# A Fourier mixer on one core: the channel transform as two products of 512 columns instead of four of 257, its evacuation given priority, and two products in one PSUM bank

## The chip, the cores and the metric

The kernel runs on one core of a Trainium2 chip. The metric is the device time of one execution in microseconds (us). The engines are TensorE (PE; PEld is its weight load), VectorE (DVE), ScalarE (ACT), GpSimd (POOL) and the DMA queues, most of them issued by SyncE (SP). PE writes its results to PSUM, which has eight banks of 512 float32 columns on 128 partitions; ACT and DVE read them from there ("evacuate").

## What is computed

Three stages follow each other; B = 8 batches, 576 positions, 512 channels (8 heads of 64).

```python
p_packed = sm_attn(p, k, v)                  # 32 queries per head over 576 positions
x = sm_attn(q, p_packed, p_packed)           # 576 queries per head over the 32

X = np.fft.fft(np.fft.fft(x, axis=1), axis=2)     # sequence, then channels
u = x + np.real(X)
un = (u - mean(u)) / np.sqrt(var(u) + 1e-6)
x2 = u + np.maximum(un @ w_ch1, 0) @ w_ch2        # 512 -> 2048 -> 512

logits = x2 @ w_gate                         # 8 experts, one chosen for each position
out = p[e] * (np.maximum(x2 @ w1[e], 0) @ w2[e])
```

Float32 accuracy is reached with float16 matmuls: a value is split in a high and a low half (hi = float16(v), lo = v - hi), and a product is three matmuls, hi*hi, hi*lo and lo*hi (PASS).

## The kernel before, in words

The generator attention(b) does the first stage and the Fourier transform of batch b, Mix the two dense layers of the second stage (L741 makes hp from ut and w1h, L749 evacuates it to ht, L761 adds w2h times ht to acc), and from about 900 us on the experts run. While Mix works on one group of tokens, attention(b) of the next batch and the splitting of the expert weights (se, so; L306 to L308) are ticked on in small steps between Mix's matmuls. Each engine works through its own instructions in order; a scheduler places them in that order at build time by priorities, and tc.high_priority moves an operation ahead (URGENT and SOON are offsets for that). A tile that an operation needs is waited for by semaphore.

The real part of a two-dimensional transform is made without the transform of x itself. x = A p_packed, with A the attention weights of 576 positions over 32 packed rows for each head, so the channel transform is applied to p_packed (256 rows of it, in two halves hf), and the sequence transform to A:

- channels(k), L466 to L477: g = p_packed times a constant table cdt of cosines (cs = 0, 257 columns) and sines (cs = 1, 257 columns). For each of four (hf, cs) a PSUM tile gp is filled by six matmuls (three passes, two halves of 64 rows), ACT casts it to float16 (L475) and DVE makes the low half (L476).
- scores2 to parts2, L484 to L547: the second attention, in three row tiles i; s is the score tile, ee the exponentials, m the sums and their reciprocals, t a partial sum made on POOL (L512), ah the split for the direct path, eo the even and odd combinations (L532 to L536) and eh their halves (L542 to L546).
- L552: a list of thirteen steps tells which of these are issued together; channels(0) to channels(3) stand in the sixth, eighth, tenth and twelfth.
- bp, L558 to L571: the sequence transform of eh, in four PSUM tiles, evacuated to bt, a part of the tile big.
- L583 to L662: for each of three row tiles t, P = bt times the cosine part of g, Q = bt times the sine part, and X, the direct attention output. ACT copies Q to qs (L634), DVE adds P and qs into ul and uu (L638 to L651) and X to those (L660). For t = 2, which has only 32 rows, P and Q already share a bank on different partitions.

All of s, gp, lp (the gate logits of earlier tokens), bp, zd, P, Q and X take their PSUM tile from one pool of two banks, in turn (psA, tag "att"; in batch 0 two of three such tiles come from another pool). So a product may begin when the tile two before it has been read:

```python
psA = ctx.enter_context(tc.tile_pool(name="psA", bufs=2, space=PSUM))
def att(nm):
    return psA.tile([128, 512], F32, tag="att", name=nm)
```

Of the kernel before, what the change touches and what calls it, by code (L numbers as in the profile page):

```python
# [8 lines left out]
F32 = mybir.dt.float32  # L9
F16 = mybir.dt.float16  # L10
I32 = mybir.dt.int32
AF = mybir.ActivationFunctionType
ALU = mybir.AluOpType
# [35 lines left out]
def prep(inputs):  # L49

    f = np.float32
    q, k, v, p = (np.asarray(inputs[n]) for n in "qkvp")
# [11 lines left out]
    o = {}  # L64
# [26 lines left out]
    def split(a):  # L91
        hi = a.astype(np.float16)
        return hi, (a - hi.astype(np.float64)).astype(np.float16)

    n = np.arange(288)[:, None]
# [26 lines left out]
    o["c3"] = c3  # L122
    c = tau[:, None]
    k2 = np.arange(257)[None, :]
    cd = np.concatenate([np.cos(2 * np.pi * ((c * k2) % 512) / 512), np.sin(2 * np.pi * ((c * k2) % 512) / 512)], 1)
    cd = np.stack(split(cd), 1)
    o["cdt"] = np.ascontiguousarray(cd.reshape(4, 128, 2, 514).transpose(1, 0, 2, 3))
    pp = np.arange(128)
    c16 = np.zeros((128, 4, 128), np.float16)
    c16[:, 0] = pp[:, None] < pp[None, :]  # L130
# [23 lines left out]
def build(tc, A, stop=None, manual=False):  # L154
    nc = tc.nc
    with ExitStack() as ctx:
        if manual:
            ctx.enter_context(tc.manual_schedule())
        _build(tc, nc, ctx, A, stop)
# [4 lines left out]
URGENT = 100  # L164
# [15 lines left out]
def _build(tc, nc, ctx, A, stop):  # L180
# [10 lines left out]
    ap = actx.enter_context(tc.tile_pool(name="ap", bufs=1, side="left"))  # L191
# [17 lines left out]
    nc.scalar.activation(warm, mhalf[0:1], AF.Exp)  # L209
    cst = ap.tile([128, 10, 290], F16, name="cst")  # L210
    c3 = ap.tile([128, 3], F32, name="c3")
    cdt = ap.tile([128, 4, 2, 514], F16, name="cdt")
    c16 = cp.tile([128, 4, 128], F16, name="c16")
    i32r = cp.tile([128, 32], F16, name="i32r")
    i32v = cp.tile([128, 32], F16, name="i32v")
# [7 lines left out]
    zt = ap.tile([128, 2, 2, 128], F16, name="zt")  # L223
# [91 lines left out]
    def attention(b):  # L315
        count = [0]

        def att(nm):
            count[0] += 1
            if b == 0 and count[0] % 3:  # L320
                return psO.tile([128, 512], F32, tag="o", name=nm)
            return psA.tile([128, 512], F32, tag="att", name=nm)
# [88 lines left out]
        for hf in range(2):  # L411
# [13 lines left out]
            n = 0  # L425
            for t in range(5):
                for (x, y) in PASS:
                    for h in range(2):
# [3 lines left out]
                                         skip_group_check=True)  # L432
# [28 lines left out]
        bt = big[:, 2304:].rearrange("p (h a c n) -> p h a c n", h=2, a=2, c=2)  # L461
        aeo = []

        g = ap.tile([128, 2, 2, 2, 257], F16, tag="g", name=f"g{b}")

        def channels(k):  # L466
            hf, cs = k % 2, k // 2
            gp = att(f"gp{b}_{k}")
            for n, (x, y) in enumerate(PASS):
                for p2 in range(2):  # L470
                    nc.tensor.matmul(gp[64 * p2:64 * p2 + 64, :257],
                                     pth[:, x, 128 * hf + 64 * p2:128 * hf + 64 * p2 + 64],
                                     cdt[:, 2 * hf + p2, y, 257 * cs:257 * cs + 257],
                                     start=n == 0, stop=n == 2, skip_group_check=True)
            nc.scalar.copy(g[:, hf, 0, cs], gp[:, :257])  # L475
            nc.vector.scalar_tensor_tensor(g[:, hf, 1, cs], gp[:, :257], 1.0, g[:, hf, 0, cs],  # L476
                                           ALU.mult, ALU.subtract)  # L477

        nrs = (128, 128, 99)
        s2s, m2s, efs, eos = {}, {}, {}, {}  # L480
# [68 lines left out]
        for steps in (((scores2, 0), (scores2, 1)), ((greatest2, 0),), ((exps2, 0), (greatest2, 1)),  # L549
                      ((scores2, 2), (sums2, 0), (exps2, 1)), ((divide2, 0), (sums2, 1), (greatest2, 2)),  # L550
                      ((channels, 0), (fold2, 0), (divide2, 1), (exps2, 2)), ((parts2, 0), (fold2, 1), (sums2, 2)),
                      ((channels, 1), (parts2, 1), (divide2, 2)), ((fold2, 2),), ((channels, 2), (parts2, 2)), (),  # L552
                      ((channels, 3),), ()):
            for fn, i in steps:
                fn(i)
            yield

        qs0 = ap.tile([128, 576], F32, tag="f32w", name=f"qs{b}_0", bufs=4)  # L558
        for k, (cs, hf) in enumerate(((0, 0), (0, 1), (1, 0), (1, 1))):
            w = 289 - cs  # L560
            bp = att(f"bp{b}_{hf}_{cs}")
            cols = slice(128 * hf, 128 * hf + 128)
            for i in range(2):
                for n, (x, y) in enumerate(PASS):
                    nc.tensor.matmul(bp[:, :w], aeo[i][:, x, cs, cols], cst[:, 4 * i + 2 * cs + y, :w],  # L565
                                     start=i + n == 0, stop=False)
            nc.tensor.matmul(bp[:, :w], aeo[2][:, 0, cs, cols], cst[:99, 8 + cs, :w], start=False, stop=True)
            nc.scalar.activation(bt[:, hf, 0, cs, :w], bp[:, :w], AF.Copy, scale=2.0 ** -4)
            nc.vector.scalar_tensor_tensor(bt[:, hf, 1, cs, :w], bp[:, :w], 2.0 ** -4, bt[:, hf, 0, cs, :w],
                                           ALU.mult, ALU.subtract)  # L570
            if k == 1:  # L571
                nc.vector.tensor_copy(zt[:, :, :, 0:1], bt[:, :, :, 0, 288:289])
            yield
            if k == 2:

                zd = att(f"zd{b}")
                n = 0
                for hf in range(2):
                    for (x, y) in PASS:
                        nc.tensor.matmul(zd[:, :257], zt[:, hf, x], g[:, hf, y, 0], start=n == 0, stop=n == 5)  # L580
                        n += 1
                nc.scalar.copy(qs0[:64, 288:545], zd[:64, :257])
                yield  # L583
        late = None
        for t in (2, 0, 1) if b % 4 == 3 else (0, 1, 2):
            s0 = 128 * t
            if t < 2:
                p0, M = 0, 128
# [4 lines left out]
            else:  # L593
                p0, M = 32 * (b % 4), 32
# [4 lines left out]
                pos = [32 * ((b + j) % 4) for j in range(4)]  # L599
            R, RQ, RL, RU = (slice(j, j + M) for j in pos)  # L600
            P = att(f"P{b}_{t}")
            Q = att(f"Q{b}_{t}") if t < 2 else P
            terms = [(hf, x, y) for hf in range(2) for (x, y) in PASS]

            def p_mm(n):
                hf, x, y = terms[n]
                nc.tensor.matmul(P[R, :257], bt[:, hf, x, 0, s0:s0 + M], g[:, hf, y, 0], start=n == 0, stop=n == 5,
                                 skip_group_check=True)

            def q_mm(n):  # L610
                hf, x, y = terms[n]
                nc.tensor.matmul(Q[RQ, :257], bt[:, hf, x, 1, s0:s0 + M], g[:, hf, y, 1], start=n == 0, stop=n == 5,
                                 skip_group_check=True)

            def x_mm(X, r, lu, n):
# [4 lines left out]
            if t < 2:  # L620
                for n in range(6):
                    p_mm(n)
                for n in range(6):
                    q_mm(n)
            else:
                X = att(f"X{b}_2")
                for n in range(6):
                    p_mm(n)
                    q_mm(n)
                    x_mm(X, RL, 0, n)  # L630
                    x_mm(X, RU, 1, n)
            yield
            qs = qs0 if t == 0 else ap.tile([128, 576], F32, tag="f32w", name=f"qs{b}_{t}", bufs=4)
            nc.scalar.copy(qs[R, :257], Q[RQ, :257])  # L634
            if t == 0:
                nc.scalar.copy(qs[0:1, :257], qs[0:1, 288:545])
            yield
# [400 lines left out]
    for n, _ in enumerate(attention(0)):  # L1038
        if n == CW0:
            while wdone[0] < CW1:  # L1040
                next(cw)
            nc.sync.dma_start(cdt, A["cdt"])
            nc.sync.dma_start(c3, A["c3"])
            nc.sync.dma_start(cst, A["cst"])
        if n == 30:
            wgf = wp.tile([128, 4, 9], F32, name="wgf")
            nc.sync.dma_start(wgf, A["wg"])
            nc.sync.dma_start(c16, A["c16"])
            nc.sync.dma_start(i32r, A["i32r"])
            nc.sync.dma_start(i32v, A["i32v"])  # L1050
            nc.sync.dma_start(c32, A["c32"])
            split(wgh[:, :, 0], wgh[:, :, 1], wgf, 64.0)
    bg.append([cw, 0.0, CW_RATE])
    mctx = ExitStack()
    M = {}
# [92 lines left out]
    for b in [0, 1, 2, "R0", 3, 4, 5, 6, "R1", 7]:  # L1148
# [16 lines left out]
        if not isinstance(b, str):  # L1165
            if b + 1 < NB:
                ga = attention(b + 1)
                bg.append([ga, 0.0, ATT_RATE])
            if b == 1:
                bg.append([ew, 0.0, EW_RATE])  # L1170
            if b == 7:
                actx.close()
                open_moe()
                drain(ew)
                drain(last)
                r0 = routing(0)
                bg.append([r0, 0.0, R0_RATE])
# [69 lines left out]
```

## Time and profile before

| what | value |
|---|---|
| median of three runs | 1500.04 us (1494.92 to 1502.7) |
| the profiled execution | 1495.18 us |
| its span, first to last instruction | 1493.4 us |
| PE, busy share of the span | 94% |
| DVE | 48% |
| ACT | 35% |
| POOL | 28% |
| mean granted TensorE clock | 0.969 |

A busy share is over the whole span. The profile names an instruction by its line, its engine and its tiles (out<-in), and tells for idle time which instruction ended it. [...]

### The profile page before, as it was taken

How to read it: one execution, taken by the hardware profiler on the slowest of the kernel's cores; microseconds unless marked ns; L12 is line 12 of the kernel's file. 1: busy time of each engine (PE TensorE's matmuls, PEld its weight loads, DVE VectorE, ACT ScalarE, POOL GpSimd, SP SyncE). 2: the span in 40 equal slices, each digit the busy share in tenths (PEclk: the TensorE clock that was granted, in tenths of full speed). 3: DMA queues.
4: the chain of work that ended last, by engine and by line, in shares of the span. 5: the costliest groups of instructions: out<-in, count | busy, mean ns of one | idle time of the engine just before them, and what ended most of it. 6: DMA issues, size and time to landing. Idle time of an engine off the chain costs nothing. (4 is left out here: it accounts for less than half of the span.)

```text
span 1493.4 us, 28983 instructions
## 1 busy us (share of the span) xinstructions
PE 1398.4 (94%) x11340; PEld 823.3 (55%) x11340; DVE 709.6 (48%) x1487; ACT 525.1 (35%) x986; POOL 418.0 (28%) x424
## 2 busy tenths in 40 slices
PE   4598898999999999899999999999899999999996
PEld 3334444544564454454444456455677777776764
DVE  5789976566544646655655654523621111111110
ACT  3343354454444545445445444211111111111111
POOL 1412125425421642442443342000211212121211
PEclk6689999999999999999999999999999999999999
DMA  7275475485466647647557455255947636783371
GB/s 272 62 234 175 143 190 156 113 235 154 118 166 178 182 119 203 159 123 224 150 140 197 115 141 163 55 196 148 248 105 235 143 98 164 237 239 71 86 231 51
DMA packets 233165, 239.72 MB, mean 161 GB/s; under 512 B 168191, under 2 KB 179583, under 8 KB 232384
## 3 DMA queue, kind: packets, MB, share of 16 engines
q1 hardware_dynamic: 226464, 217.62, 53.6%
q0 software_dynamic: 6560, 20.19, 4.1%
q8 instruction: 91, 1.49, 0.4%
q14 instruction: 50, 0.41, 0.1%
HBM read 267.38 MB, written 53.74 MB: 215 GB/s over the span
## 5 line engine op out<-in xcount | busy, mean ns | idle before, releaser
L761 PE MATMUL acc<-w2h,ht 128*128 128x512 f16 x1728 | 417.0, 383 | 0.0
L741 PE MATMUL hp<-ut,w1h 128*128 128x512 f16 x1536 | 370.5, 382 | 6.0 <-DMA ut<-unh 5.2
L741 PEld LDWEIGHTS <-w1h 128*128 128x128 f16 x1920 | 183.6, 98 | 186.3 <-issue 19.5
L761 PEld LDWEIGHTS <-ht 128*128 128x128 f16 x1728 | 166.5, 99 | 188.8 <-issue 13.0
L1109 PE MATMUL ehp<-xgt,w1b 128*128 128x128 f16 x3936 | 230.7, 219 | 1.7 <-DMA w1b<-WS 1.2
L1109 PEld LDWEIGHTS <-w1b 128*128 128x128 f16 x3936 | 224.4, 98 | 12.7 <-DMA w1b<-WS 1.4
L308 POOL TENSOR_TENSOR so<-se,so 128x512 f16<-128x512 f32 x128 | 149.3, 1171 | 269.4 <-ACT so L307 251.1
L1127 PE MATMUL eo<-w2b,hx 128*128 128x512 f16 x984 | 219.2, 379 | 0.0
L1117 DVE SCALAR_TENSOR_TENSOR hx<-ehp,hx 128x512 f16<-128x512 f32 x82 | 56.7, 691 | 338.5 <-ACT hx L1116 338.4
L749 DVE SCALAR_TENSOR_TENSOR ht<-hp,ht 128x512 f16<-128x512 f32 (+1 forms) x160 | 101.3, 633 | 142.9 <-ACT ht L748 142.4
L748 ACT ACTIVATE ht<-hp 128x512 f16<-128x512 f32 (+1 forms) x160 | 88.1, 550 | 229.9 <-PE hp L741 229.8
L1127 PEld LDWEIGHTS <-hx 128*128 128x128 f16 x984 | 94.5, 98 | 106.1
L1135 POOL DMA_INDIRECT out<-ys,sidx x41 | 41.6, 1015 | 328.0 <-ACT ys L1134 323.5
L1116 ACT ACTIVATE hx<-ehp 128x512 f16<-128x512 f32 x82 | 48.9, 597 | 181.0 <-PE ehp L1109 176.6
L1134 ACT ACTIVATE ys<-eo,scl 128x512 f32<-128x512 f32 x41 | 28.2, 687 | 179.1 <-PE eo L1127 179.1
L307 ACT CAST so<-se 128x512 f16<-128x512 f32 x128 | 77.8, 615 | 13.0 <-DMA WS<-so 9.8
L306 ACT ACTIVATE se<-se 128x512 f32<-128x512 f32 x128 | 77.5, 622 | 0.2
L1077 POOL DMA_INDIRECT xg<-XS,gidx x41 | 42.2, 1030 | 125.5 <-DVE tfe L1031 53.9
L346 POOL TENSOR_TENSOR qh<-q,qh 128x1420 f16<-128x1420 f32 x12 | 34.6, 2884 | 63.3 <-ACT qh L345 53.3
L741 PE MATMUL hp<-utr,w1h 128*128 128x256 f16 x384 | 47.1, 272 | 0.0
L696 POOL TENSOR_TENSOR unh<-un,unh 128x512 f16<-128x512 f32 x32 | 37.7, 1192 | 21.8 <-ACT unh L695 21.8
L565 PE MATMUL bp<-cst,eh 128*128 128x289 f16 (+1 forms) x192 | 31.8, 305 | 9.8 <-ACT eh L542 6.2
(289 smaller groups left out, 1382.0 us busy)
## 6 DMA issues: line engine op xcount, KB each, us to landing
w1b<-WS SPq DMA_DIRECT2D x156, 512.0 KB
w2b<-WS SPq DMA_DIRECT2D x156, 512.0 KB
se<-in_w SPq DMA_DIRECT2D x64, 512.0 KB
WS<-so SPq DMA_DIRECT2D x128, 256.0 KB
sw<-in_wc SPq DMA_DIRECT2D x32, 512.0 KB
q<-in_qd SPq DMA_DIRECT2D x16, 710.0 KB
v<-in_vd SPq DMA_DIRECT2D x16, 640.0 KB
k<-in_kd SPq DMA_DIRECT2D x16, 576.0 KB
```

Of the source, the lines that this page charges most:

```text
L306: nc.scalar.activation(st[:, a], st[:, a], AF.Copy, scale=64.0 if k < 4 else 256.0)
L307: nc.scalar.copy(so[:, 0], st[:, a])
L308: nc.gpsimd.tensor_tensor(so[:, 1], st[:, a], so[:, 0], op=ALU.subtract)
L741: nc.tensor.matmul(hp[:, :ntok], w1h[:, f, c, x], ut[:, 4 * y + c, :ntok], start=n == 0, stop=n == 11)
L748: pace[1] = nc.scalar.activation(ht[:, 0, :ntok], hp[:, :ntok], AF.Relu).ins
L749: pace[0] = nc.vector.scalar_tensor_tensor(ht[:, 1, :ntok], hp[:, :ntok], 0.0, ht[:, 0, :ntok], ALU.max, ALU.subtract).ins
L761: nc.tensor.matmul(self.acc[j], ht[:, x, 128 * j:128 * j + 128], w2h[:, f, y], start=f == 0 and n == 0, stop=f == 15 and n == 2)
L1077: nc.gpsimd.indirect_dma_start(out=g_, out_offset=None, in_=XS[0:rows], in_offset=bass.IndirectOffsetOnAxis(ap=gidx[:, b:b + 1], axis=0), ...
L1109: nc.tensor.matmul(hp[:, cols], w1b[b % RB][:, 2 * c + fg, x, cols], xt[b][:, 4 * y + c], start=n == 0, stop=n == 11, skip_group_check=True)
L1116: nc.scalar.activation(ht[:, fg, 0], hp, AF.Relu)
L1117: nc.vector.scalar_tensor_tensor(ht[:, fg, 1], hp, 0.0, ht[:, fg, 0], ALU.max, ALU.subtract)
L1127: nc.tensor.matmul(op, h[:, f // 4, x, 128 * (f % 4):128 * (f % 4) + 128], w2b[b % RB][:, f, y], start=n == 0, stop=n == 23)
```

## The change

The sine columns 0 and 256 are zero for every channel. The change leaves them out of the table: 257 cosine and 255 sine columns are 512, one full bank. channels(hf) makes one product of 512 columns for each half, and there are two of them, in the sixth and the tenth step. Their evacuation by ACT and DVE stands under high_priority(URGENT). P takes columns 0 to 256 of a bank and Q columns 257 to 511 of the same one, so that Q takes no tile of its own from the pool for t < 2. The two columns of qs that Q no longer fills are set to zero by POOL, and qs is taken before the products.

```diff
@@ -122,9 +122,10 @@
     o["c3"] = c3
     c = tau[:, None]
     k2 = np.arange(257)[None, :]
-    cd = np.concatenate([np.cos(2 * np.pi * ((c * k2) % 512) / 512), np.sin(2 * np.pi * ((c * k2) % 512) / 512)], 1)
+    cd = np.concatenate([np.cos(2 * np.pi * ((c * k2) % 512) / 512),
+                         np.sin(2 * np.pi * ((c * k2[:, 1:256]) % 512) / 512)], 1)
     cd = np.stack(split(cd), 1)
-    o["cdt"] = np.ascontiguousarray(cd.reshape(4, 128, 2, 514).transpose(1, 0, 2, 3))
+    o["cdt"] = np.ascontiguousarray(cd.reshape(4, 128, 2, 512).transpose(1, 0, 2, 3))
     pp = np.arange(128)
     c16 = np.zeros((128, 4, 128), np.float16)
     c16[:, 0] = pp[:, None] < pp[None, :]
@@ -209,7 +210,7 @@
     nc.scalar.activation(warm, mhalf[0:1], AF.Exp)
     cst = ap.tile([128, 10, 290], F16, name="cst")
     c3 = ap.tile([128, 3], F32, name="c3")
-    cdt = ap.tile([128, 4, 2, 514], F16, name="cdt")
+    cdt = ap.tile([128, 4, 2, 512], F16, name="cdt")
     c16 = cp.tile([128, 4, 128], F16, name="c16")
     i32r = cp.tile([128, 32], F16, name="i32r")
     i32v = cp.tile([128, 32], F16, name="i32v")
@@ -461,20 +462,19 @@
         bt = big[:, 2304:].rearrange("p (h a c n) -> p h a c n", h=2, a=2, c=2)
         aeo = []
 
-        g = ap.tile([128, 2, 2, 2, 257], F16, tag="g", name=f"g{b}")
-
-        def channels(k):
-            hf, cs = k % 2, k // 2
-            gp = att(f"gp{b}_{k}")
+
+        g = ap.tile([128, 2, 2, 512], F16, tag="g", name=f"g{b}")
+
+        def channels(hf):
+            gp = att(f"gp{b}_{hf}")
             for n, (x, y) in enumerate(PASS):
                 for p2 in range(2):
-                    nc.tensor.matmul(gp[64 * p2:64 * p2 + 64, :257],
+                    nc.tensor.matmul(gp[64 * p2:64 * p2 + 64],
                                      pth[:, x, 128 * hf + 64 * p2:128 * hf + 64 * p2 + 64],
-                                     cdt[:, 2 * hf + p2, y, 257 * cs:257 * cs + 257],
-                                     start=n == 0, stop=n == 2, skip_group_check=True)
-            nc.scalar.copy(g[:, hf, 0, cs], gp[:, :257])
-            nc.vector.scalar_tensor_tensor(g[:, hf, 1, cs], gp[:, :257], 1.0, g[:, hf, 0, cs],
-                                           ALU.mult, ALU.subtract)
+                                     cdt[:, 2 * hf + p2, y], start=n == 0, stop=n == 2, skip_group_check=True)
+            with tc.high_priority(offset=URGENT):
+                nc.scalar.copy(g[:, hf, 0], gp)
+                nc.vector.scalar_tensor_tensor(g[:, hf, 1], gp, 1.0, g[:, hf, 0], ALU.mult, ALU.subtract)
 
         nrs = (128, 128, 99)
         s2s, m2s, efs, eos = {}, {}, {}, {}
@@ -549,8 +549,7 @@
         for steps in (((scores2, 0), (scores2, 1)), ((greatest2, 0),), ((exps2, 0), (greatest2, 1)),
                       ((scores2, 2), (sums2, 0), (exps2, 1)), ((divide2, 0), (sums2, 1), (greatest2, 2)),
                       ((channels, 0), (fold2, 0), (divide2, 1), (exps2, 2)), ((parts2, 0), (fold2, 1), (sums2, 2)),
-                      ((channels, 1), (parts2, 1), (divide2, 2)), ((fold2, 2),), ((channels, 2), (parts2, 2)), (),
-                      ((channels, 3),), ()):
+                      ((parts2, 1), (divide2, 2)), ((fold2, 2),), ((channels, 1), (parts2, 2)), (), (), ()):
             for fn, i in steps:
                 fn(i)
             yield
@@ -577,7 +576,7 @@
                 n = 0
                 for hf in range(2):
                     for (x, y) in PASS:
-                        nc.tensor.matmul(zd[:, :257], zt[:, hf, x], g[:, hf, y, 0], start=n == 0, stop=n == 5)
+                        nc.tensor.matmul(zd[:, :257], zt[:, hf, x], g[:, hf, y, :257], start=n == 0, stop=n == 5)
                         n += 1
                 nc.scalar.copy(qs0[:64, 288:545], zd[:64, :257])
                 yield
@@ -599,17 +598,20 @@
                 pos = [32 * ((b + j) % 4) for j in range(4)]
             R, RQ, RL, RU = (slice(j, j + M) for j in pos)
             P = att(f"P{b}_{t}")
-            Q = att(f"Q{b}_{t}") if t < 2 else P
+
+            Q = P[RQ, 257:512] if t < 2 else P[RQ, 1:256]
+            qs = qs0 if t == 0 else ap.tile([128, 576], F32, tag="f32w", name=f"qs{b}_{t}", bufs=4)
+            nc.gpsimd.memset(qs[R, 0:257:256], 0.0)
             terms = [(hf, x, y) for hf in range(2) for (x, y) in PASS]
 
             def p_mm(n):
                 hf, x, y = terms[n]
-                nc.tensor.matmul(P[R, :257], bt[:, hf, x, 0, s0:s0 + M], g[:, hf, y, 0], start=n == 0, stop=n == 5,
+                nc.tensor.matmul(P[R, :257], bt[:, hf, x, 0, s0:s0 + M], g[:, hf, y, :257], start=n == 0, stop=n == 5,
                                  skip_group_check=True)
 
             def q_mm(n):
                 hf, x, y = terms[n]
-                nc.tensor.matmul(Q[RQ, :257], bt[:, hf, x, 1, s0:s0 + M], g[:, hf, y, 1], start=n == 0, stop=n == 5,
+                nc.tensor.matmul(Q, bt[:, hf, x, 1, s0:s0 + M], g[:, hf, y, 257:], start=t == 2 and n == 0, stop=n == 5,
                                  skip_group_check=True)
 
             def x_mm(X, r, lu, n):
@@ -630,8 +632,7 @@
                     x_mm(X, RL, 0, n)
                     x_mm(X, RU, 1, n)
             yield
-            qs = qs0 if t == 0 else ap.tile([128, 576], F32, tag="f32w", name=f"qs{b}_{t}", bufs=4)
-            nc.scalar.copy(qs[R, :257], Q[RQ, :257])
+            nc.scalar.copy(qs[R, 1:256], Q)
             if t == 0:
                 nc.scalar.copy(qs[0:1, :257], qs[0:1, 288:545])
             yield
```

In the rows below, L numbers of the change are one higher than before. The first place is DVE in batch 2, around the evacuations of gp; ee, eo, ah and eh belong to the second attention's third row tile (and its second), ht to Mix. Before:

```order
L520 TENSOR_TENSOR ee2_2_2359<-ee2_2_2359,m2_2_2_2357 99x512
L534 SCALAR_TENSOR_TENSOR eo2_2_2456<-ee2_2_2359,c3_93 99x256
L528 SCALAR_TENSOR_TENSOR ah2_1_2407<-ee2_1_2295,ah2_1_2407 128x512
L476 SCALAR_TENSOR_TENSOR g2_2221<-gp2_1_2424,g2_2221 128x257
L535 TENSOR_SCALAR eo2_2_2456<-eo2_2_2456,c3_93 99x256
L528 SCALAR_TENSOR_TENSOR ah2_2_2452<-ee2_2_2359,ah2_2_2452 32x512
L546 SCALAR_TENSOR_TENSOR eh2_2_2479<-eh2_2_2479,c3_93,eo2_2_2456 99x512
L476 SCALAR_TENSOR_TENSOR g2_2221<-gp2_2_2470,g2_2221 128x257
L749 SCALAR_TENSOR_TENSOR ht4_8_2485<-hp4_8_2448,ht4_8_2485 128x512
L476 SCALAR_TENSOR_TENSOR g2_2221<-gp2_3_2496,g2_2221 128x257
```

The same place in the change:

```order
L520 TENSOR_TENSOR ee2_2_2325<-ee2_2_2325,m2_2_2_2323 99x512
L534 SCALAR_TENSOR_TENSOR eo2_2_2413<-ee2_2_2325,c3_93 99x256
L528 SCALAR_TENSOR_TENSOR ah2_1_2373<-ee2_1_2261,ah2_1_2373 128x512
L535 TENSOR_SCALAR eo2_2_2413<-eo2_2_2413,c3_93 99x256
L528 SCALAR_TENSOR_TENSOR ah2_2_2409<-ee2_2_2325,ah2_2_2409 32x512
L546 SCALAR_TENSOR_TENSOR eh2_2_2436<-eh2_2_2436,c3_93,eo2_2_2413 99x512
L477 SCALAR_TENSOR_TENSOR g2_2187<-gp2_1_2427,g2_2187 128x512
L750 SCALAR_TENSOR_TENSOR ht4_8_2442<-hp4_8_2405,ht4_8_2442 128x512
```

The second of the two evacuations now stands directly behind eh; the one between ah and L535 is gone, and so are the two behind eh. The first evacuation stands ahead of these rows in both.

The second place is PE in the same batch, from the third gp of four before, and from the second of two in the change; lp is the gate product, bp the first sequence transform, and what a row waits for stands behind it. Before:

```order
L471 MATMUL gp2_2_2470<-cdt_94,pth2_2199 64x257 [waits DVE_49]
...
L741 MATMUL hp4_8_2448<-ut1_1558,w1h_127 128x512
...
L761 MATMUL acc4_1911<-w2h_128,ht4_6_2275 128x512
...
L471 MATMUL gp2_3_2496<-cdt_94,pth2_2199 64x257 [waits DVE_49]
...
L761 MATMUL acc6_1913<-w2h_128,ht4_6_2275 128x512
...
L778 MATMUL lp2_2519<-wgh_110,xt2_2370 128x18 [waits DVE_49]
...
L565 MATMUL bp2_0_0_2535<-cst_92,eh2_0_2404 128x289 [waits DVE_49]
```

The same place in the change:

```order
L472 MATMUL gp2_1_2427<-cdt_94,pth2_2165 64x512 [waits PE_49]
...
L742 MATMUL hp4_8_2405<-ut1_1523,w1h_127 128x512
...
L762 MATMUL acc4_1877<-w2h_128,ht4_6_2241 128x512
...
L779 MATMUL lp2_2467<-wgh_110,xt2_2336 128x18 [waits DVE_49]
...
L564 MATMUL bp2_0_0_2483<-cst_92,eh2_0_2370 128x289 [waits DVE_49]
```

The second gp waits for no evacuation of a gp any more. The bank of lp is that of the first gp, the bank of bp that of the second.

The third place is DVE in batch 0, ahead of the first row of eo, where m and ee belong to the first row tile and wgh is the split of the gate weights. Before:

```order
L519 RECIPROCAL m2_0_0_336<-m2_0_0_336 128x16
L518 TENSOR_SCALAR m2_0_1_341<-m2_0_1_341 128x16
L476 SCALAR_TENSOR_TENSOR g0_317<-gp0_1_403,g0_317 128x257
L520 TENSOR_TENSOR ee0_0_338<-ee0_0_338,m2_0_0_336 128x512
L519 RECIPROCAL m2_0_1_341<-m2_0_1_341 128x16
```

The same place in the change:

```order
L519 RECIPROCAL m2_0_0_336<-m2_0_0_336 128x16
L518 TENSOR_SCALAR m2_0_1_341<-m2_0_1_341 128x16
L263 SCALAR_TENSOR_TENSOR wgh_110<-wgf_430,wgh_110 128x4x9
L520 TENSOR_TENSOR ee0_0_338<-ee0_0_338,m2_0_0_336 128x512
L519 RECIPROCAL m2_0_1_341<-m2_0_1_341 128x16
```

The split of wgh has taken the place of the second evacuation, which now stands six rows higher, directly behind the first.

## Rows read from the trace of the kernel before

**Rows 1.** The page's first part: busy time, share of the span, instructions by engine

```profile
PE 1398.4 (94%) x11340; PEld 823.3 (55%) x11340; DVE 709.6 (48%) x1487; ACT 525.1 (35%) x986; POOL 418.0 (28%) x424
```

**Rows 2.** Waits of PE: who waited for whom, us in total, times, longest

```profile
PE gp L471 <- DVE g L476: 17.5, 6, 4.5
...
PE bp L565 <- DVE g L476: 1.4, 2, 0.8
```

**Rows 3.** Timeline of PE, batch 2: start, length, instructions [idle before and its releaser]

```profile
246.43 0.52 PE L471 MATMUL gp<-cdt,pth 128*64 128x257 f16 x6
246.88 0.82 PE L741 MATMUL hp<-ut,w1h 128*128 128x512 f16 x3
...
252.78 0.86 PE L471 MATMUL gp<-cdt,pth 128*64 128x257 f16 x6 [3.78 <-DVE g L476]
...
257.38 0.22 PE L778 MATMUL lp<-wgh,xt 128*128 128x18 f16 x1
...
257.64 0.94 PE L741 MATMUL hp<-ut,w1h 128*128 128x512 f16 x3
258.42 0.79 PE L565 MATMUL bp<-cst,eh 128*128 128x289 f16 x5
```

**Rows 4.** Timeline of DVE, batch 2

```profile
248.53 3.26 DVE L534 SCALAR_TENSOR_TENSOR eo<-ee,c 99x256 f32<-99x256 f32 x1
251.71 0.68 DVE L528 SCALAR_TENSOR_TENSOR ah<-ee,ah 128x512 f16<-128x512 f32 x1
252.31 0.41 DVE L476 SCALAR_TENSOR_TENSOR g<-gp,g 128x257 f16<-128x257 f32 x1
252.65 0.34 DVE L535 TENSOR_SCALAR eo<-eo,c 99x256 f32<-99x256 f32 x1
...
253.72 0.75 DVE L546 SCALAR_TENSOR_TENSOR eh<-eh,c,eo 99x512 f16<-99x512 f16 x1
254.38 0.42 DVE L476 SCALAR_TENSOR_TENSOR g<-gp,g 128x257 f16<-128x257 f32 x1
```

**Rows 5.** Timeline of POOL, batch 2, and all of L534 (ns min/median/max, first and last start)

```profile
248.56 0.73 POOL L536 TENSOR_TENSOR eo<-ee 99x256 f32<-99x256 f32 x1 [1.26 <-DVE ee L520]
249.24 1.15 POOL L544 TENSOR_TENSOR eh<-eo,eh 128x512 f16<-128x512 f32 x1
250.35 1.15 POOL L308 TENSOR_TENSOR so<-se,so 128x512 f16<-128x512 f32 x1
...
L534 DVE SCALAR_TENSOR_TENSOR eo<-ee,c x8: 467/2078/3257, 52.1 to 838.7; 99x256 f32<-99x256 f32 x8
```

**Rows 6.** Two stretches behind a wait (busy by engine, PEclk, DMA, GB/s), and the second's wait

```profile
252.78:258.42 5.64, 5.64 (x27) 2.30 (x27) 3.31 (x8) 3.82 (x8) 1.61 (x3) 0.54 0.70 178
...
481.25:485.00 3.75, 3.75 (x43) 2.15 (x44) 1.38 (x1) 2.63 (x2) 0.15 (x1) 1.00 1.11 378
...
481.25 0.92 PE L429 MATMUL pps<-vhl,et 128*64 128x128 f16 x26 [2.58 <-DMA et<-ehl]
```

**Rows 7.** Timelines of PE and DVE in the last of the five such batches, batch 7

```profile
835.79 0.52 PE L471 MATMUL gp<-cdt,pth 128*64 128x257 f16 x6
...
841.79 0.86 PE L471 MATMUL gp<-cdt,pth 128*64 128x257 f16 x6 [3.42 <-DVE g L476]
...
846.57 0.91 PE L565 MATMUL bp<-cst,eh 128*128 128x289 f16 x6
...
842.72 0.75 DVE L546 SCALAR_TENSOR_TENSOR eh<-eh,c,eo 99x512 f16<-99x512 f16 x1
```

**Rows 8.** Groups by line: a DVE operation of 512 columns on PSUM, a POOL memset

```profile
L1117 DVE SCALAR_TENSOR_TENSOR hx<-ehp,hx 128x512 f16<-128x512 f32 x82 | 56.7, 691 | 338.5 <-ACT hx L1116 338.4
...
L389 POOL MEMSET ehl<- x16: 196/204/272, 3.8 to 778.2; 128x128 f16 x16
```

**Rows 9.** Timelines of DVE and PE, batch 0

```profile
51.06 1.14 DVE L262 SCALAR_TENSOR_TENSOR wgh<-wgf,wgh 128x36 f16<-128x36 f32 x1
...
46.82 0.67 PE L565 MATMUL bp<-cst,eh 128*128 128x289 f16 x2 [5.92 <-ACT eh L542]
```

## The prediction

> **What bounds the kernel now.** I read the page first: TensorE (PE) is busy for 94% of the span [rows 1], so a change gains only where PE stands still. Next the list of what PE waited for: the largest single entry is the channel transform, 17.5 us in six waits for VectorE's evacuation of an earlier product (gp <- DVE g), and the same evacuation holds PE twice more for 1.4 us at bp [rows 2]. Then I laid the timelines of PE, DVE and POOL side by side at batch 2, the first batch of the steady part, to see why that evacuation is late.
>
> At 252.78 the third product had been issued (246.43) and the fourth stood 3.78 us; it wants the bank of the second product [rows 3]. That bank is released by the evacuation at 252.31, which takes only 0.41 us but stands behind eo (L534), which took 3.26 us [rows 4]. While L534 ran, POOL ran three operations back to back, from 248.56 to 251.50, and DVE's next operation started at 251.71 [rows 5]. L534 has eight executions, from 0.467 to 3.257 us [rows 5]: it ends when POOL's run ends. So the wait is not made by the size of the evacuations; it comes from a VectorE operation that is held up, and all that is queued behind it.
>
> Batches 3, 5, 6 and 7 show the same picture, with 3.43, 4.54, 1.26 and 3.42 us at the same product; batch 4 has none. Behind such a wait the clock is also low: in the 5.64 us after 252.78 the granted clock was 0.54, against 1.00 after a wait of 2.58 us that ended at 481.25 [rows 6]. From the fourth product to the first bp, PE needs about 3.3 us at full clock: 0.45 for the product, 1.32 and 0.66 and 0.66 for twelve 512-column products (three take from 246.88 to 247.54) and 0.26 at most for lp [rows 3]. It took 5.64 in batch 2 and 4.78 in batch 7 [rows 3, 7], so the clock cost 2.3 and 1.5 us there; by the same subtraction 1.5 in batch 3 and 2.4 in batch 5, **7.7 in all**.
>
> **The change, part by part, at batch 2.**
>
> *Two wide products for four narrow ones.* A group of six 257-column matmuls takes 0.45 us (246.43 to 246.88) and three 512-column matmuls take 0.66 [rows 3]; the two 64-column halves of a group overlap, so a wide group is three such steps and a fixed part of 0.1, 0.77 us. Four times 0.45 less two times 0.77 is 0.26 us of PE per batch.
>
> *The evacuations.* Each wide one costs more than a narrow one: VectorE's 512-wide operation on PSUM takes 0.691 us [rows 8], against 0.41 for the narrow one [rows 4]. From start to start VectorE's are 0.34 apart now (252.31 to 252.65) and would be about 0.6. Four times 0.34 against two times 0.6 is equal within 0.2 us, so VectorE gains nothing by itself.
>
> *Where PE now waits.* In the order of the change the second product no longer needs a g evacuation: its bank was used by the scores, long read. The wait of 3.78 us goes. But bp needs the bank of the second product, and VectorE's order puts that evacuation directly behind eh (L546); nothing of what precedes it, L534 included, is moved or shortened. PE reaches bp after the work it had from the third product on: 0.45 + 0.66 + 1.32 and the 3.3 from above, less 0.26, is 5.45 us, so at 246.43 + 5.45 = 251.88. The bank comes free so: L546 started at 253.72 [rows 4]; without the narrow evacuation ahead of it (252.31 to 252.65) it starts at 253.38; the next operation started 0.66 behind it, so the wide evacuation starts at 254.04 and ends after 0.6 to 0.69. PE goes on at 254.7 instead of 258.42: 3.7 us earlier, **with a wait of 2.8 us at bp in place of 3.78 us at gp**. bp's seventh matmul needs eh of L546 anyway, so even a free bank would give little over half a microsecond more. URGENT does not change that: with it the order still has this evacuation behind eh, on DVE as on ACT.
>
> For batch 7 the same steps give an arrival at 835.79 + 5.45 = 841.24, a release at 842.72 - 0.34 + 0.66 + 0.6 = 843.6, a wait of 2.3 and 3.0 us won against 846.57 [rows 7]. Batches 3, 5 and 6 give 3.0, 3.9 and 1.4 won, with waits of 2.4, 3.45 and 2.6. The five batches win 3.7 + 3.0 + 3.9 + 1.4 + 3.0 = **15.0 us** before the clock behind the new waits is paid; batch 4, which has no wait, wins 0.26.
>
> *The clock behind the new waits.* Waits of 3.4 us and more were all followed by a low clock, the waits of 1.26 and of 2.58 us were not [rows 3, 6, 7]. The new ones lie between 2.3 and 3.45. The bounds are nothing (no clock lost) and 1.5 to 2.4 each, some 8.5 in all (1.7 on average). I take three of five: 2.4 behind the longest, 1.5 behind two others, 5.4 us. [...]
>
> *L534 itself.* I leave its 3.26 us as they are, since the POOL operations behind it stand in the same order in the change. [...]
>
> *P and Q in one bank, and the memsets.* P and Q keep their matmuls; two columns less are nothing. X finds its bank free earlier, but among PE's waits of 1 us and more none is at X; I take 0. The 24 new memsets on POOL are bounded by nothing and by the nearest memset, 0.204 us [rows 8], 0.6 us per batch; POOL was busy for 28% of the span, the memsets precede their use by a whole product, and nothing on POOL waits in the order for PE. I take 0; their price if that cover goes is 0.2 us each ahead of a POOL operation.
>
> *The first two batches.* In batch 0 the order moves the split of wgh, 1.14 us on VectorE [rows 9], ahead of the division whose result feeds the first bp, and takes one narrow evacuation (0.34) out; the two wide ones fall where VectorE waits for POOL. So the first bp, which already waits 5.92 us for eh [rows 9], comes 0.8 to 1.1 us later. In batch 1 the longer of bp's two waits for g, 0.8 us [rows 2], has its cause moved, and I take that as won. Together nothing, within 1.5 us either way.
>
> **Sum.** 15.0 + 0.26 - 5.4 + 0 = 9.9 us less. The profiled execution took 1495.18 us, and would take 1485.3; the median of the three runs shown is 1500.04, near 5 us above it, so against that median the forecast is **1490.0 us**. Nothing behind 900 us is touched.
>
> **Rivals.**
> *A: the clock holds.* If none of the shorter waits lowers the clock, nothing is taken off the 15.0: 1500.04 - 15.3 = 1484.8. For it: the wait of 2.58 us that kept 1.00. Against it: two of the new waits are near 3 us or above. If POOL's run also released L534 early, up to the 13.55 us of new waits would go too, and the time would be 1471; nothing in the order asks for that.
> *B: slower.* POOL's run behind eo grows by one split of expert weights (1.15 us, as the last of the three [rows 5]) and by the new memset (0.2), because the cast before them comes sooner. L534 then lasts that much longer and all behind it is later, so bp in six batches starts 1.35 later, 8.1 us, and every wait is long enough for the clock to be lost, 6 x 2.4 = 14.4; against 15.3 won this is +7.2, and with the first bp 1.1 later +8.3: 1508. It decides from the point at which L534 lasts over 3.3 us in most batches. For it: the number of operations in the run already varies from one to three. Against it: POOL's order has no more operations between eo and the next memset than before.
> *C: the wait changes its place and pays in full.* The clock is lost behind all five: 15.3 - 8.5 = 6.8, and with the first bp 1.1 later 5.7: 1494.3. For it: every wait of 3.4 us or more paid. [...]
> *D: no difference from the edit at all* would need the four evacuations to have been off the path; the 17.5 us of [rows 2] exclude it; I give it no chance of its own.
>
> **How the numbers follow.** The forecast has 0.48, A 0.18 (0.03 of it for the far end), C 0.22, B 0.12. The forecast's own spread is about 3 us to either side (one wait more or less that pays, 1.5 us at the start). A measurement of this kernel can tell 0.5%, 7.5 us, from no change, so the border is at 1492.5. Most of the forecast (0.37) and nearly all of A (0.17) lie below it: faster 0.54. C and the rest of the forecast lie within: 0.34 with a small part of B. Slower takes the rest of B, 0.12. The range reaches from a little below A to a little above C and the lower half of B: 1481 to 1502.
>
> **What would show it.** Right: gp <- DVE g is gone from PE's list; bp (L564) waits for DVE's g (L477) once in batches 2, 3, 5, 6 and 7, 2.3 to 3.5 us each; L534 still takes 2 to 3.3 us; the clock is 0.5 to 0.7 behind two or three of these waits and 1.00 behind the others; the first bp of batch 0 starts near 47.7. Wrong: a bp wait under 1 us (then L534 is not what holds the evacuation), or a g evacuation that itself waits for ScalarE's cast over 0.5 us, or a wait for POOL's memset.

## The result, and the profile after

The change takes 1482.68 us (median of four, 1480.97 to 1483.95) against 1498.2 before (four, 1494.92 to 1502.7). The ratio is 0.9902, with a 95% interval of 0.9879 to 0.9926: 15 us less (11 to 18), which is more than the 0.5% that the prediction takes as its bound. The forecast was 10 us less than a median of 1500.04, so 1490.0, with a range of 1481 to 1502; the measured time lies near the range's lower end. The profiled execution took 1483.01 us, 12.2 less than the profiled one before.

PE's waits after, in the order of [rows 2]; gp <- DVE g has left the list:

```profile
PE bp L564 <- DVE g L477: 13.9, 5, 3.4
...
PE gp L472 <- DVE ee L502: 2.1, 1, 2.1
```

The five waits on PE's timeline, in batches 2, 3, 5, 6 and 7, answer to the waits of gp in [rows 3, 7]:

```profile
256.75 1.61 PE L564 MATMUL bp<-cst,eh 128*128 128x289 f16 x6 [2.65 <-DVE g L477]
...
364.31 0.91 PE L564 MATMUL bp<-cst,eh 128*128 128x289 f16 x6 [2.50 <-DVE g L477]
...
621.01 0.91 PE L564 MATMUL bp<-cst,eh 128*128 128x289 f16 x6 [3.41 <-DVE g L477]
...
728.91 0.90 PE L564 MATMUL bp<-cst,eh 128*128 128x289 f16 x6 [2.80 <-DVE g L477]
...
834.83 0.90 PE L564 MATMUL bp<-cst,eh 128*128 128x289 f16 x6 [2.51 <-DVE g L477]
```

The forecast had 2.8, 2.4, 3.45, 2.6 and 2.3. The stall was moved and shortened, not removed. What it is worth shows on PE's timeline as the time from a batch's first gp to its first bp, and from there to its first P:

| batch | gp to bp before | after | less | forecast | bp to P before | after |
|---|---|---|---|---|---|---|
| 2 | 17.64 | 13.73 | 3.9 | 3.7 | 9.96 | 11.61 |
| 3 | 16.50 | 13.58 | 2.9 | 3.0 | 10.05 | 10.06 |
| 4 | 12.66 | 12.09 | 0.6 | 0.26 | 9.96 | 9.96 |
| 5 | 18.46 | 14.49 | 4.0 | 3.9 | 9.97 | 11.65 |
| 6 | 15.17 | 13.89 | 1.3 | 1.4 | 9.96 | 9.95 |
| 7 | 16.43 | 13.60 | 2.8 | 3.0 | 10.06 | 10.05 |

The last two columns hold the price of the clock: in two batches, 2 and 5, PE needed 1.65 and 1.68 us more for the same work behind the wait. The windows of 3.3 us behind the five waits say the same: a granted clock of 0.50 in batch 2 and 0.65 in batch 5, and of 1.00 in batches 3, 6 and 7. Batches 2 and 6 (PEclk, the granted clock as a share of full speed, is the third number from the end):

```profile
256.75:260.05 3.30, 3.30 (x11) 1.61 (x11) 1.01 (x4) 2.02 (x5) 1.66 (x3) 0.50 0.78 206
...
728.91:732.21 3.30, 3.30 (x22) 2.09 (x22) 1.63 (x5) 2.03 (x5) 1.16 (x1) 1.00 0.67 215
```

DVE and POOL in batch 2 answer to [rows 4, 5]. L534 is shorter (2.15 us against 3.26); POOL's third operation no longer follows the second directly, a memset of the change (L604, 0.10 us) stands between them. But then L535 takes 1.24 us (0.34 before). Batch 5 shows the same; in batches 3, 6 and 7 L534 takes 2.15 us (2.14, 2.01 and 2.14 before), and L535 0.34 to 0.35 as before.

```profile
250.70 2.15 DVE L534 SCALAR_TENSOR_TENSOR eo<-ee,c 99x256 f32<-99x256 f32 x1
...
253.38 1.24 DVE L535 TENSOR_SCALAR eo<-eo,c 99x256 f32<-99x256 f32 x1
...
255.35 0.75 DVE L546 SCALAR_TENSOR_TENSOR eh<-eh,c,eo 99x512 f16<-99x512 f16 x1
256.01 0.68 DVE L477 SCALAR_TENSOR_TENSOR g<-gp,g 128x512 f16<-128x512 f32 x1
```

```profile
250.73 0.73 POOL L536 TENSOR_TENSOR eo<-ee 99x256 f32<-99x256 f32 x1 [1.19 <-DVE ee L520]
251.41 1.16 POOL L544 TENSOR_TENSOR eh<-eo,eh 128x512 f16<-128x512 f32 x1
252.63 0.10 POOL L604 MEMSET qs<- 128x2 f32 x1
252.72 1.75 POOL L309 TENSOR_TENSOR so<-se,so 128x512 f16<-128x512 f32 x1
```

The cast on ACT was not what was late there: it ended at 255.80, and DVE came to the evacuation at 256.01, directly behind eh.

```profile
255.22 0.58 ACT L476 CAST g<-gp 128x512 f16<-128x512 f32 x1
```

### The profile page after: what moved, and what is told of

Its sections match the earlier page's. It is cut to its first block, busy times and chain, and to the rows that moved or that the text cites. A ratio compares the mean times of both kernels' runs of the same rounds, so it can differ in the third digit from the quotient of the medians.

```text
span 1481.2 us, 28789 instructions
## 1 busy us (share of the span) xinstructions
PE 1391.4 (94%) x11244; PEld 816.6 (55%) x11244; DVE 703.4 (47%) x1471; ACT 522.9 (35%) x970; POOL 424.2 (29%) x448
## 5 line engine op out<-in xcount | busy, mean ns | idle before, releaser
L762 PE MATMUL acc<-w2h,ht 128*128 128x512 f16 x1728 | 409.7, 380 | 0.0
L564 PE MATMUL bp<-cst,eh 128*128 128x289 f16 (+1 forms) x192 | 33.3, 313 | 24.7 <-DVE g L477 13.9
```

Source lines behind the costliest of these rows:

```text
L762: nc.tensor.matmul(self.acc[j], ht[:, x, 128 * j:128 * j + 128], w2h[:, f, y], start=f == 0 and n == 0, stop=f == 15 and n == 2)
```

## The experiments

Theory: the two wide products carry the gain, and what is left is DVE held up by POOL's run. Rivals: the priority, or the shared bank. All but e13 start from the change; ratios are to the kernel before on the same chip, with their 95% intervals. The change was not run again beside them, so a difference to its 1482.68 us is one of two medians; where the interval of a ratio overlaps the change's (0.9879 to 0.9926), the difference is not clear of noise.

**The parts of the change.**

```diff
 e1_no_priority, e3_wide_only:
-            with tc.high_priority(offset=URGENT):
 e2_q_own_bank, e3_wide_only:
-            Q = P[RQ, 257:512] if t < 2 else P[RQ, 1:256]
+            Q = att(f"Q{b}_{t}")[RQ, 1:256] if t < 2 else P[RQ, 1:256]
...
 e4_share_only: channels(k) for k in 0..3 with 257 or 255 columns, in the steps of before, no priority
```

> The change without the priority of the g evacuations. Theory (the two wide products carry the gain: the wait leaves gp and comes back, shorter, at bp): from batch 2 on the order is the same, so bp waits for DVE's g five times, 2.3 to 3.5 us each, and the time is 10 to 16 us under before, like the change's. The priority only moves work in batches 0 and 1: within 3 us of the change. Rival (the priority carries the gain): within 4 us of before, with g evacuations late in every batch.

It took 1480.15 us, a ratio of 0.9893 (0.9874 to 0.9913): not told apart from the change, as the theory had it. bp waits for g five times, 14.2 us in all.

> The change with Q in a bank of its own again. Theory: P and Q in one bank is worth nothing, because X was not waited for: 10 to 16 us under before, within 3 us of the change, the five waits at bp as in the change. Rival (the shared bank frees a bank for X and carries part of the gain): 5 us or more over the change, with waits of PE at X or Q in the list.

It took 1487.7 us, 0.9956 (0.9935 to 0.9977). The five waits at bp are there (14.0 us), yet it lies 5 us over the change, clear of noise: the theory's waits with the rival's time.

> Only the two products of 512 columns: no priority, Q in its own bank. Theory: still 9 to 16 us under before, the waits gp <- DVE g gone and bp <- DVE g at 13 to 15 us in five waits. Rival (the parts work together): less than half of the gain, under 7 us.

It took 1480.99 us, 0.9908 (0.9882 to 0.9933), with the waits of the change:

```profile
PE bp L563 <- DVE g L476: 13.9, 5, 3.4
```

> Four narrow products as before (257 and 255 columns), but P and Q in one bank. Theory: within 4 us of before; the list of waits still has gp <- DVE g with 15 to 19 us in five or six waits, and the clock is low behind most of them. Rival (sharing carries the gain): 8 us or more under before.

It took 1499.24 us, 1.0006 (0.9985 to 1.0028), with the wait at gp as before (17.5 in six there):

```profile
PE gp L475 <- DVE g L479: 15.8, 6, 3.4
```

The two wide products alone bring the whole gain; the priority adds nothing, and sharing the bank alone brings nothing. Why priority with Q in its own bank (e2) loses 5 us that neither loses alone stays open; its list of waits shows none at Q or X. Its profile places the loss ahead of batch 2, where priority moves work: from batch 0's first gp to batch 2's first PE took 205.0 us, against 201.8 in the change, 202.8 in e1 and 197.0 in e3.

**What holds the evacuation up.**

```diff
 e5_pool_longer
             nc.gpsimd.tensor_tensor(eo[:, 256:], ef[:, :256], ef[:, 256:], op=ALU.subtract)
+            if i == 2:
+                nc.gpsimd.tensor_tensor(eo[:, 256:], ef[:, :256], ef[:, 256:], op=ALU.subtract)
 e7_eo_on_dve
-            nc.gpsimd.tensor_tensor(eo[:, 256:], ef[:, :256], ef[:, 256:], op=ALU.subtract)
+            (nc.gpsimd if i < 2 else nc.vector).tensor_tensor(eo[:, 256:], ef[:, :256], ef[:, 256:], op=ALU.subtract)
 e11_no_l518
-            nc.vector.tensor_scalar(m2[:, 1], m2[:, 1], 2.0 ** -10, 1e-9 * 2.0 ** -10, ALU.mult, ALU.add)
...
-            nc.vector.tensor_tensor(ee, ee, m2[:, 1].unsqueeze(2).to_broadcast([nrs[i], 16, 32]), op=ALU.mult)
+            nc.vector.scalar_tensor_tensor(ee, ee, 1024.0, m2[:, 1].unsqueeze(2).to_broadcast([nrs[i], 16, 32]),
+                                           ALU.mult, ALU.mult)
```

> The change with POOL's subtraction for the third row tile of eo done twice (the same values written again), so that POOL's run beside L534 is 0.73 us longer; the order on PE, DVE and ACT is the change's, row for row. Theory (L534 ends when POOL's run ends, and all up to the second g evacuation stands behind it): L534 goes from 2.15 to about 2.9 us in batches 2, 3, 5, 6 and 7, the waits of bp for g from 14 to 17 to 18 us, and the time is 3 to 9 us over the change's (3.7 of waits, the rest clock). Rival (the evacuation is late by its own queue or by the cast on ScalarE, POOL only happens to be busy): L534 and the waits as before, the time within 2 us of the change.

It took 1487.9 us, 0.9927 (0.9899 to 0.9956), 5 us over the change, but the intervals overlap. The waits went from 13.9 to 15.8 us: the sign is the theory's, the size half of it, and the place is not. In batches 2, 3, 5 and 7 L534 fell to 1.04 us and L535 rose to 1.92. Over all eight the means were 1.69 and 0.64 us in the change, and here:

```profile
L534 DVE SCALAR_TENSOR_TENSOR eo<-ee,c 99x256 f32<-99x256 f32 x8 | 9.1, 1131 | 0.7
...
L535 DVE TENSOR_SCALAR eo<-eo,c 99x256 f32<-99x256 f32 x8 | 11.6, 1446 | 0.1
```

> The change with the second half of eo of the third row tile made by DVE instead of POOL, so that POOL has nothing released at the moment L534 starts. Theory: L534 falls from 2.15 us to 0.5 to 1.1, the added DVE operation costs 0.35 to 0.5, and the waits of bp fall from 14 us to 4 to 9; 3 to 12 us under the change. [...]

It took 1485.48 us, 0.9925 (0.9904 to 0.9946), not told apart from the change; the theory's gain did not come. The waits fell to 11.3 us in four, not to 4 to 9. L534 fell as expected, but L518, of 16 columns, now lasted until POOL's run ended, 3.02 us against 1.90 in the change. Batch 2:

```profile
247.40 3.02 DVE L518 TENSOR_SCALAR m<-m 99x16 f32<-99x16 f32 x1
...
249.24 1.16 POOL L544 TENSOR_TENSOR eh<-eo,eh 128x512 f16<-128x512 f32 x1
...
251.55 0.48 DVE L534 SCALAR_TENSOR_TENSOR eo<-ee,c 99x256 f32<-99x256 f32 x1
```

> The change without the operation L518 (1.9 us in batch 2, of 16 columns): the sum of exponentials is inverted without the scale 2^-10 and without the 1e-9 that is added to it, and the scale is put into the next multiplication, so the small number is left out of the computation. Theory (the hold-up belongs to POOL's run and not to the operation, so it moves to the next one that meets it, as it did when eo was moved): L519 or eo last longer, and the waits of bp stay at 10 to 14 us; within 4 us of the change. Rival (L518 itself is the cost): the waits fall by 1.7 us each to 5 to 7 us, 6 to 12 us under the change.

It took 1476.82 us, 0.9867 (0.9842 to 0.9891), 6 us under the change, which is more than the theory's 4 and the least of the rival's; the intervals overlap. The waits are 11.1 us, as the theory said. With L518 gone the multiplication behind it takes its place (0.69 us in the change, where it was without the scale):

```profile
245.10 2.13 DVE L519 SCALAR_TENSOR_TENSOR ee<-ee,m 99x512 f32<-99x512 f32 x1
```

So it is not one operation that costs; as far as these runs show it, the run on POOL does, through the operation that is long beside it: L534 with 2.15 us in the change, L518 with 3.02 in e7, L519 with 2.13 in e11. Not every operation is held: beside POOL's eh the reciprocal took its usual 0.25 us in e11 (at 244.81), and L517 its usual 0.29 in e7 (at 247.08) and in the change (at 247.35, eh from 247.28 to 248.44). The next runs take part of POOL's work away.

```diff
 e8_pool_quiet, e9_early_quiet, e12_quiet_rate, e13_before_quiet
-            if it[0] is ew and phase[0] < EWS:
+            if it[0] is ew and (phase[0] < EWS or quiet[0]):
...
+            quiet[0] = (exps2, 0) in steps or quiet[0]
             for fn, i in steps:
                 fn(i)
             yield
+        quiet[0] = False
 e12_quiet_rate, e13_before_quiet
-EW_RATE = 1.3
+EW_RATE = 1.5
```

> The change, with the splitting of expert weights held back from the exponentials of the second attention to its end, in every batch, so that POOL has none of those 1.15 us subtractions beside DVE's stretch from L518 to eh; the rest of POOL's work stays. Theory (DVE stands still as long as POOL's run lasts, whichever of its operations meets it): two of POOL's operations, 2.3 us, are gone from the stretch, and the five waits of bp for g fall from 14 us to 4 to 9; 4 to 12 us under the change. Rival (DVE's own work makes the wait): waits of 12 to 15 us, the time within 3 us of the change, or over it for the weights that come later.

It took 1491.37 us, 0.9959 (0.9935 to 0.9983). The waits fell as expected and no clock was lost behind them (bp to P took 9.96 to 10.06 us in batches 2 to 7), but the whole was 9 us over the change. The gain was given back behind batch 7: from its first P to the first expert product PE needed 189.7 us against 173.4, 6.0 of the 16.3 more in a wait for the routing. The weights came late; their last cast started at 986.9 against 933.0. In batch 2 L534 and L535 (here L535 and L536) took 1.04 and 0.35 us, against 2.15 and 1.24 in the change:

```profile
247.47 1.04 DVE L535 SCALAR_TENSOR_TENSOR eo<-ee,c 99x256 f32<-99x256 f32 x1
248.55 0.35 DVE L536 TENSOR_SCALAR eo<-eo,c 99x256 f32<-99x256 f32 x1
```

```profile
PE tabe L1001 <- DVE bve L1013: 6.0, 1, 6.0
...
PE bp L567 <- DVE g L478: 5.3, 5, 1.7
```

The edit holds back the weights' steps on ACT as well, and no run separates the two. For POOL speak the lengths of DVE's operations, and e5, which made POOL's run alone longer and the waits with it.

> The change with the expert weights held back during the second attention, and their pace outside it raised from 1.3 to 1.5, so that they are ready when they were in the change. Theory (held weights won 14 us up to batch 7 and lost them again because the weights came late): bp <- DVE g at 4 to 7 us in the steady part as with the weights only held, and 10 to 18 us under the change, near 1468. Rival (the won time is lost wherever the weights go, because DVE and ScalarE are held up elsewhere): within 5 us of the change.

It took 1476.12 us, 0.9857 (0.9842 to 0.9872), 6.6 under the change: clear of noise, less than the theory's 10 and more than the rival's 5. The loss behind batch 7 is gone (173.6). A part of what is missing lies ahead of batch 2: from batch 0's first gp to batch 2's first PE took 205.9 us, against 201.8 in the change and 200.6 in e8.

```profile
PE bp L567 <- DVE g L478: 7.2, 5, 2.5
```

> The kernel before, four narrow products, with the expert weights held back and paced in the same way. Theory (POOL's run is what makes the evacuations late, before as after): gp <- DVE g falls from 17.5 us to 4 to 9, and the time is 8 to 16 us under before, so that what the change adds to it is less than the 15 us that it brings alone. Rival (the four narrow products need the change to profit): gp <- DVE g at 14 us or more, within 5 us of before.

It took 1484.6 us, 0.9904 (0.9886 to 0.9922), 12.7 us under before. With four narrow products that is by the ratio as much as the change itself wins, and when POOL is quiet the change adds only 8.5 us to it (e12, on the same chip). The wait at gp fell as the theory said, but a part of it went to lp, which takes the bank of the third product (1.6 us before): the waits for g at gp, lp and bp together fell from 20.5 to 11.6 us.

```profile
PE lp L781 <- DVE g L477: 5.4, 5, 1.7
...
PE gp L472 <- DVE g L477: 4.8, 5, 1.1
```

**Where the evacuation stands.**

```diff
 e6_early_products, e9_early_quiet
-                      ((channels, 0), (fold2, 0), (divide2, 1), (exps2, 2)), ((parts2, 0), (fold2, 1), (sums2, 2)),
-                      ((parts2, 1), (divide2, 2)), ((fold2, 2),), ((channels, 1), (parts2, 2)), (), (), ()):
+                      ((channels, 0), (channels, 1), (fold2, 0), (divide2, 1), (exps2, 2)), ((parts2, 0), (fold2, 1), (sums2, 2)),
+                      ((parts2, 1), (divide2, 2)), ((fold2, 2),), ((parts2, 2),), (), (), ()):
```

> The change with both products issued one behind the other in the sixth step, so that the second evacuation stands ahead of L534 on DVE. Theory (bp's seventh matmul needs eh, which stands behind L534 as well): no wait bp <- DVE g in batches 2 to 7, but a wait at L566 for DVE's eh of 1.3 to 2.5 us in four or five of them; 0 to 8 us under the change, most of it chance of the clock. Rival (the place of the evacuation is what costs, rival A's far end): no waits of either kind over 0.5 us, 12 us or more under the change.

It took 1472.64 us, 0.9837 (0.9817 to 0.9857): 10 us under the change, **the fastest of all runs**. That lies between the theory and the rival: bp waits for eh less than the theory had (4.0 us in five), the wait for g is gone, and the second gp waits for the reading of the scores:

```profile
PE gp L472 <- DVE ee L502: 8.6, 6, 2.1
...
PE bp L566 <- DVE eh L546: 4.0, 5, 1.4
```

> Both products in the sixth step and the expert weights held back as well. Theory: the waits at L566 for eh (4.0 us with the early products alone) fall under 2, the waits of gp for ee (8.6) stay, and the time is 0 to 5 us under that of the early products alone, which was 1472.64. Rival (nothing is left to win at eh, and the held weights collide with DVE elsewhere): 0 to 6 us over it.

It took 1488.81 us, 0.9936 (0.9915 to 0.9957), 16 us over e6, more than theory or rival had. bp's waits for eh fell to 2.2 us in two, and those of gp stayed at 8.6. It pays the late weights as e8 does (tabe <- DVE bve 5.6 us), so it does not tell what both would bring at the right pace; that was not run.

## Why the prediction was right, step by step

- *Where PE waits.* Right, to 0.2 us in each of the five batches; the 15.0 us to be won before the clock came out as 3.9 + 2.9 + 4.0 + 1.3 + 2.8 = 14.9 (the table). e3 and e4 show that the two wide products bring it.
- *L534 stays as it is.* Right in batches 3, 6 and 7. In batches 2 and 5 it was wrong in the place: L534 and L535 took 2.15 and 1.24 us instead of 3.26 and 0.34. That their sum stayed near (3.39 against 3.60) no step had foreseen; there it was luck.
- *The clock behind the new waits.* Three of five and 5.4 us were forecast; that it would be three was the author's estimate between none and all, and no run shows that number. In the change's profile two paid, 3.3 us. The waits of e1, e2 and e3 are the same to 0.3 us, and there five, two and four paid, 9.0, 4.4 and 7.8 us (bp to P over that of before). So 13 of 20 paid, 6.1 us per execution: the term was about right, and the change's profile was the cheapest of the four.
- *The profiled execution* was to take 1485.3 us and took 1483.01. Its gain of 12.2 is the 14.9, and 0.6 in batch 4, and 1.9 where two other waits of PE became shorter (at 481.25, 2.58 to 1.48; at 594.61, 0.70 gone), less the 3.3 of clock and 2.2 by which batch 2 began later; some 0.3 are left over.
- *From the profile to the median.* This is the step that missed most. It took the median to lie near 5 us above the profiled execution, as before (1500.04 and 1495.18); after the change the two agree (1482.68 and 1483.01). Of the 7.3 us between 1490.0 and the measurement this makes 5.0, the profile 2.3. One profile of each kernel does not tell why.
- *The first two batches.* Forecast as nothing, within 1.5 us, with the first bp 0.8 to 1.1 later: right. From batch 0's first gp PE took 9.53 us to its first bp against 8.71, and 201.8 to batch 2's first gp against 202.7. Without priority (e1, e3) the first bp came after 7.75. That it started at 50.79 and not near 47.7, and batch 2 later by 2.2, comes from ahead of the change's part: the first gp started at 41.26 against 38.12. That start lies between 38.1 and 41.3 in all profiles, at 41.27 in e13, with four narrow products.
- *"Even a free bank would give little over half a microsecond more."* Too low, and e6 shows it. From the first gp to the first bp its five batches are shorter by a further 1.1 to 2.2 us (13.73 to 11.72 in batch 2). A part comes back behind bp, in waits for eh and for the evacuation of the bp before; to the first P, less the price of the clock, 0.3 to 1.6 are left, 1.1 in batches 3 and 7. The step left out that bp's six matmuls before eh, 0.74 us, can run while eh is still on its way, beside the 0.66 of the evacuation.
- *P and Q in one bank, the memsets at 0.* Right for the time: e4 is 1.0006 with both in it. The memset took 0.098 us, half the nearest one's 0.204. That one of them now stands in POOL's run where L534 ends was not foreseen, and no run takes the memsets out of the change.
- *Rival A* (the clock holds) would have been 1484.8, *C* (it pays in full) 1494.3. The measurement is near A's time but not by A's mechanism, since two of the five waits paid; that it lies there is luck. *B* did not come: in the change no L534 lasted over 2.16 us.

## What to carry to other kernels

When a wait names an evacuation of 0.4 us, read what stands ahead of it on its engine, and what the other engines run then; here two products fewer moved the wait to the next bank in turn (17.5 us at gp before, 13.9 at bp after), and it could be worked out from the order where it lands. Put the evacuation ahead of the stretch with the long operations (e6), or keep background work of the other engine out of that stretch and pay its pace back elsewhere (e12): the two were worth 10 and 7 us here. Taking a single long operation away won little where the next one was long in its place (e7 and e11, neither clear of noise against the change).

## What the runs showed of the hardware that was not expected

The clock behind one and the same wait differs between runs. Behind bp's wait of 2.65 us in batch 2 (2.66 in e2) the next 3.3 us had a granted clock of 0.59, 1.00 and 0.60 in e1, e2 and e3, in this order below, and 0.50 in the change:

```profile
256.23:259.53 3.30, 3.30 (x13) 1.72 (x13) 0.99 (x4) 2.02 (x5) 1.61 (x3) 0.59 0.72 221
```

```profile
258.71:262.01 3.30, 3.30 (x22) 2.08 (x22) 0.86 (x3) 1.94 (x6) 1.39 (x3) 1.00 0.76 214
```

```profile
251.46:254.76 3.30, 3.30 (x13) 1.61 (x13) 0.86 (x3) 1.94 (x5) 1.39 (x3) 0.60 0.77 204
```

Where it fell, the stretch from bp to P took 1.3 to 2.9 us longer (9.96 to 11.25 in batch 2 of e1, 9.96 to 12.88 in its batch 6). Only the longest wait, 3.4 us in batch 5, was followed by it in all four. So PE's waits repeat to 0.1 us from run to run (one of the twenty differs by 0.3), and what follows them does not.

One and the same DVE operation on 16 columns (L518) lasted 0.13 to 3.01 us in the kernel before and 0.13 to 1.90 in the change. Its longest ended with a run of POOL: at 512.57 in batch 4 before, POOL's run at 512.54, and at 249.57 in batch 2 of the change, POOL's run at 249.54. L534 ended 0.27 to 0.29 us behind a POOL operation of 512 columns in batches 2, 3, 5, 6 and 7 of both kernels (251.79 and 251.50 in batch 2 before, 252.85 and 252.57 after). It had started 0.03 us ahead of POOL's eo in nine of these ten (248.53 and 248.56 in batch 2 before [rows 4, 5], 250.70 and 250.73 after) and 0.11 behind it in batch 6 before (732.04 and 731.93), and it lasted through three operations of POOL in batch 2 before. So the traces agree with a hold-up of DVE by POOL's run; what makes it they do not show, and the starts that they show do not tell which engine is held.
